# Small tiles of an attention and feed-forward kernel declared in another order, so that the transposed activations lie 64 bytes past the weight slots modulo 256

## Chip, cores and metric

One core of a Trainium2 chip runs the whole program. The metric is the device time of one execution in microseconds (us). Engines are named as in the profile: PE is the matmul engine and PEld its loading of stationary operands, DVE the vector engine, ACT the scalar engine, POOL the GpSimd engine, SP the engine that issues most DMAs. The on-chip memory (SBUF) has 128 partitions; a tile takes the same byte range in each of them, and "address" below is the byte within a partition.

## What is computed

The input x has 2048 rows of 640. It is layer-normed, goes through a local attention and a feed-forward network side by side, and the two are multiplied and added to x:

```python
x = A_x
xn = _layernorm(x, axis=-1)
s = _A_ref(xn, A_wqkv, A_wo)         # 32 heads of 20; each row looks at itself and 7 rows back, step 2
g = _silu(_B_ref(xn, B_w1, B_w2))    # silu(silu(xn @ w1) @ w2), w1 640x1536, w2 1536x640
return x + s * g
```

Attention is `softmax(q . k * 20**-0.5) . v` over 8 positions, then a product with `wo` (640x640); `wqkv` is 640x1920. All is float32.

## The kernel before

**Precision by halves.** Every matmul operand is split into a high and a low half of type fp32r, and each product is made as three matmuls: high by high, low by high, high by low. So one 128x128 piece of a stationary operand is loaded, and one row of up to 512 columns is streamed past it (the moving operand), for each of 3357 matmuls. While a matmul streams, the next one's stationary operand is loaded.

**Staging.** The 2048 rows are taken in four groups of 512 (`groups`), each of four tiles of 128 rows. For each group, PE does these phases in turn:

- `qkv_phase`: four quarters of heads. Per quarter 5 chunks `c` x 4 tiles `t` x 3 matmuls (lines 737 to 739): stationary is a 128-column slice of the transposed normed rows (`TH`, high, or `TL`, low), moving is a slot of the weight ring, 512 columns in three quarters and 384 in the last. In the first group the first quarter is done by `first_quarter` (line 676).
- `wo_phase` for the group before (lines 766 and 768, in `tm_mm`): stationary is a slice of `TH`/`TL`, which now hold the transposed attention output; moving is a weight slot, 384 columns and then 256. That is 120 matmuls. For the last group `wo_last` does it at the end, with 120 matmuls again (15 of them on line 864).
- `ffn_phase`: six times two `up` (lines 882 to 884, 15 matmuls each: stationary is a 128-column piece of a weight slot, moving a whole row of `TH`/`TL`, 512 columns) and one `down` (lines 766 and 768 again, 48 matmuls of 384 and 256 columns: stationary is a slice of `SH` or `SL`, the halves of silu's result, moving a weight slot).

So `TH`/`TL` are stationary in the QKV and `wo` phases and moving in `up`; the weight ring is the other operand everywhere.

**Other engines.** ACT copies matmul results out of PSUM (lines 525, 528), makes silu (888, 889) and exp (588), and copies transposed rows into place (487) and into their high half (471). DVE does the attention itself (571, 574, 609, 614), the low halves (472, 890) and layer norm. POOL issues the loads of already split weights into the ring of 7 slots (line 402), SP the other DMAs. The order of work on ACT, DVE, POOL and SP comes from a planner (`Weave`) that gives every operation a cost and writes one fixed order; no tile's address enters into it. PE's order is that of the code.

**Where tiles lie.** All SBUF tiles come from one pool with one buffer, and are laid one behind the other in the order of their declaration, from address 16512 on; each starts at a multiple of 32 bytes. A slice of 128 columns of `TH` or `SH` begins at a multiple of 512 bytes within its tile, a row `c` of `TH` at a multiple of 2048, a weight slot's low half at 2048, 2560 or 1536; the slots lie 5120 bytes apart. Modulo 256 all pieces of a tile thus start where the tile starts.

Of the kernel before, what the change touches and what calls it, by code (L numbers as in the profile page):

```python
# [8 lines left out]
F32 = mybir.dt.float32  # L9
# [5 lines left out]
P = 128  # L15
S, D, F, H, DH = 2048, 640, 1536, 32, 20
W = 8
# [3 lines left out]
HQ = H // NQ  # L21
CQ = HQ * DH
J = 8
T = 4
# [29 lines left out]
def tsl(t):  # L54
    return slice(t * P, (t + 1) * P)
# [157 lines left out]
def local_attention_silu_ffn(ctx: ExitStack, tc: tile.TileContext, x, wqkv, wo, w1, w2, out):  # L213
    nc = tc.nc
    pool = lambda name, bufs, **kw: ctx.enter_context(tc.tile_pool(name=name, bufs=bufs, **kw))
    sb = pool("sb", 1)
# [16 lines left out]
    def tiles(name, n, shape, dtype=F32):  # L233
        return [sb.tile(shape, dtype, name=f"{name}{i}") for i in range(n)]

    ident = sb.tile([P, P], F32, name="ident")
    epst = sb.tile([P, 1], F32, name="epst")
    MV = sb.tile([P, T, 2], F32, name="mv")
    ST = [sb.tile([P, 2, 6], F32, name="st0")]
    TH = tiles("th", 2, [P, DC, TOK], F32R)  # L240
    TL = tiles("tl", 2, [P, DC, TOK], F32R)
    WR = tiles("w", RING, [P, 2 * D], F32R)
    ST.append(sb.tile([P, 2, 6], F32, name="st1"))
    SH = tiles("sh", 2, [P, TOK], F32R)
    SL = tiles("sl", 2, [P, TOK], F32R)
    SD = sb.tile([P, 2, T], F32, name="sd")
    mask = sb.tile([P, T, W], F32, name="mask")
    M = tiles("m", 2, [P, T, HQ])
    Z = tiles("z", 2, [P, 2, T, HQ])
    KV = tiles("kv", NQ, [P, 2, HALO + T, CQ])  # L250
    Q = sb.tile([P, T, D], F32, name="q")
# [36 lines left out]
    def dve(n, fn, reads, writes, prio, lock=False):  # L288
        add("DVE", dv(n), fn, reads, writes, prio, lock)

    def act(n, fn, reads, writes, prio, table=None):
        add("ACT", ac(n), fn, reads, writes, prio, table=table)

    def pe(dur, fn, reads, writes):
        add("PE", dur, fn, reads, writes)
        clock[0] += dur
# [49 lines left out]
    def width(u):  # L346
        return qcols(u[1]) + 2 * CQ if u[0] == "q" else D
# [41 lines left out]
    def w_load():  # L389
# [5 lines left out]
        n = width(u)  # L395
        r = WR[s]
        both = r[:, :2 * n]
# [27 lines left out]
    def w_next(*want):  # L425
# [4 lines left out]
        s, n = i % RING, width(want)  # L430
        return WR[s][:, :n], WR[s][:, n:2 * n], ("wh", s), ("wl", s)

# [10 lines left out]
    def ln_stats(t, after=()):  # L443
        st = ST[t % 2]
        ks = ("st", t % 2)
        for k in range(2):
            dve(320, lambda k=k: nc.vector.bn_stats(out=st[:, k, :], in_=XIN[:, t, k * 320:(k + 1) * 320]),
                [("xin", t), *after], [ks + (k,)], 1)
        dve(60, lambda: nc.vector.bn_aggr(out=MV[:, t, :], in_=st), [ks + (0,), ks + (1,)], [("mv", t)], 1)

    def ln_rstd(a, b, at=1, after=()):
        n = range(a, b)
        act(b - a, lambda: nc.scalar.activation(SD[:, 0, a:b], MV[:, a:b, 1], AF.Sqrt, bias=epst, scale=1.0),
            [("mv", t) for t in n] + list(after), [("sd", t) for t in n], 0, "sqrt")
        dve(10, lambda: nc.vector.reciprocal(out=SD[:, 1, a:b], in_=SD[:, 0, a:b]),
            [("sd", t) for t in n], [("rs", t) for t in n], at)

    def ln_apply(t):
        dve(320, lambda: nc.vector.tensor_scalar(
            out=XIN[:, t, :], in0=XIN[:, t, :], scalar1=MV[:, t, 0:1], scalar2=SD[:, 1, t:t + 1],  # L460
            op0=OP.subtract, op1=OP.mult), [("rs", t), ("mv", t)], [("xin", t)], 1, lock=True)
# [3 lines left out]
    def split_sb(c, keys, i, prio=0.4):  # L465
# [3 lines left out]
        kh, kl = t_keys(i, [c], kinds=["th"]), t_keys(i, [c], kinds=["tl"])  # L469
        hi, lo = (w[i][:, c, :].rearrange("p (t i b) -> p t i b", t=T, i=NB) for w in (TH, TL))  # L470
        act(TOK, lambda: nc.scalar.activation(hi, v, AF.Copy), keys, kh, prio)
# [84 lines left out]
    def halo_keys(q, ws=(0, 1)):  # L556
        return [("halo", q, tag, a, w) for tag in (1, 2) for a in (0, 112) for w in ws] + [
            ("halo", q, 3, 0), ("halo", q, 4, 0)] + [("kv", q, t) for t in range(T)]
# [4 lines left out]
    def scores(g, q):  # L563
        i = q % 2
        l, e, m, kv, qq = L[i], E[i], M[i], KV[q], Q[:, :, q * CQ:(q + 1) * CQ]
        hk = halo_keys(q, (0,))
# [54 lines left out]
    def first_quarter(i):  # L621
# [10 lines left out]
        def begin(t):  # L632
# [3 lines left out]
            for k in range(2):  # L636
                cs = slice(k * 320, (k + 1) * 320)
                kx = ("xin", t) if t or k else ("xin", t, "a")
                dve(320, lambda k=k, cs=cs: nc.vector.bn_stats(out=st[:, k, :], in_=XIN[:, t, cs]), [kx], [ks + (k,)], at)
            dve(60, lambda: nc.vector.bn_aggr(out=MV[:, t, :], in_=st), [ks + (0,), ks + (1,)], [("mv", t)], at)  # L640
            ln_rstd(t, t + 1, at)
            for j, (a, b) in enumerate(PARTS if not t else ((0, DC),)):
                cs = slice(a * P, b * P)
                dve((b - a) * (64 if not t else 85), lambda cs=cs: nc.vector.tensor_scalar(
                    out=XIN[:, t, cs], in0=XIN[:, t, cs], scalar1=MV[:, t, 0:1], scalar2=SD[:, 1, t:t + 1],
                    op0=OP.subtract, op1=OP.mult), [("rs", t), ("mv", t), ("xin", t)], [("xn", t, j)] if not t else [("xn", t, 0), ("xn", t, 1)],
                    at, lock=True)

        def turn(t):
# [10 lines left out]
            for a, b, j, tp, kp in parts:  # L660
                v = tp[:, :(b - a) * P].rearrange("p (c n) -> p c n", n=P)
                dve((b - a) * P, lambda a=a, b=b, v=v: nc.vector.tensor_tensor(
                    out=TL[i][:, a:b, tsl(t)], in0=v, in1=TH[i][:, a:b, tsl(t)].bitcast(F32), op=OP.subtract),
                    [kp] + t_keys(i, range(a, b), [t], ["th"]), t_keys(i, range(a, b), [t], ["tl"]),
                    1.6 if a and not t else 0)

        def products(t, steps):

            o, kp = ps[t]
            for k, c in steps:  # L670
                x, kx = (TL, "tl") if k == 1 else (TH, "th")
                wh, wl, kh, kl = ws[c]
# [45 lines left out]
    def qkv_phase(g, i, io):  # L718
# [4 lines left out]
        for q in range(NQ):  # L723
            if g == 0 and q == 0:
                ps = first_quarter(i)
            else:
                ps = [bank() for t in range(T)]
                for c in range(DC):
                    wh, wl, kh, kl = w_next("q", q, c)
                    n = width(("q", q, c))  # L730
                    for t in range(T):
                        o, kp = ps[t]

                        def unit(c=c, t=t, o=o, wh=wh, wl=wl, n=n):
                            o = o[:, :n]
                            hi, lo = TH[i][:, c, tsl(t)], TL[i][:, c, tsl(t)]
                            nc.tensor.matmul(o, hi, wh, start=c == 0, stop=False)  # L737
# [16 lines left out]
    def t_keys(i, cs, ts=range(T), kinds=("th", "tl")):  # L754
        return [(k, i, c, t) for k in kinds for c in cs for t in ts]
# [6 lines left out]
    def tm_mm(banks, t, st, w, first, last, cols=(0, 1)):  # L762
        a, b = banks
        h = t % 2
        if 0 in cols:
            nc.tensor.matmul(a[t][0][:, :CA], st, w[:, :CA], start=first, stop=last)  # L766
        if 1 in cols:
            nc.tensor.matmul(b[t // 2][0][:, h * CB:(h + 1) * CB], st, w[:, CA:], start=first and h == 0,  # L768
                             stop=last, skip_group_check=True)
# [18 lines left out]
    def wo_phase(g, i):  # L788
        banks = tm_banks(True)
        a, b = banks  # L790
        for c in range(DC):
# [6 lines left out]
            for t in range(T):  # L798
                def small(c=c, t=t, wh=wh):
                    tm_mm(banks, t, TL[i][:, c, tsl(t)], wh, False, c == DC - 1)  # L800
                pe(TM, small, t_keys(i, [c], [t], ["tl"]) + [kh], [a[t][1], b[t // 2][1]])
# [13 lines left out]
    def wo_last(g, i):  # L815
# [21 lines left out]
        def steps(cs):  # L837
            return [(TH, c, k) for c in cs for k in (0, 1)] + [(TL, c, 0) for c in cs]

# [139 lines left out]
```

## Time and profile before

| | |
|---|---|
| time, median of 3 runs | 621.21 us (621.16 to 621.39) |
| the profiled execution's own time | 621.44 us |
| its span, first to last instruction | 619.7 us |
| PE busy, share of the span | 614.2 us, 99% |
| DVE busy | 561.3 us, 91% |
| ACT busy | 309.5 us, 50% |
| POOL busy | 112.8 us, 18% |
| granted PE clock | 0.999 |

The span is what instructions cover; the 1.7 us between it and the execution's time lie around it. A matmul's busy time in the profile overlaps with that of its neighbours (a 512-column one shows 389 ns, but the next one starts some 227 ns later), so what one matmul costs is read from starts: the start of a phase's first matmul, the start of the next phase's first, and the count of matmuls between.

### The profile page before, as it was taken

Reading aid. Unit: us, or ns where it says so; the run is one execution under the profiler, and the core shown is the slowest. Engines: PE = TensorE matmul, PEld = TensorE weight load, DVE = VectorE, ACT = ScalarE, POOL = GpSimd, SP = SyncE. Lnnn points to the kernel's source line nnn. Section 1 sums busy time; section 2 is a strip of 40 time slices with the busy share of each in tenths; the row PEclk is TensorE's granted clock in tenths of the full one; section 3 lists DMA queues with packets and bytes.
Section 4 is the critical chain, followed back from the end, with each engine's and each line's share of the span. In section 5 each row is a group of like instructions: output and inputs, shape, how many; then the busy total and the mean of one; then the engine's idle time right before and its main releaser. Section 6 shows DMA issues by size and latency. Waiting matters only on the chain.

```text
span 619.7 us, 9092 instructions
## 1 busy us (share of the span) xinstructions
PE 614.2 (99%) x3357; PEld 555.3 (90%) x3357; DVE 561.3 (91%) x581; ACT 309.5 (50%) x651; POOL 112.8 (18%) x168
## 2 busy tenths in 40 slices
PE   8999999999999999999999999999999999999997
PEld 7889999998889999999888999999888999998997
DVE  6558999999989997999998999999979999899974
ACT  5435558937376213951944502583396316152750
POOL 4510000011101133111212233311121213311100
PEclk9999999999999999999999999999999999999999
DMA  8999999866999998764699999855579998956642
GB/s 248 343 287 324 354 345 391 356 236 186 304 322 348 328 356 259 238 195 139 203 242 251 340 333 304 276 176 163 169 202 278 251 334 277 316 179 202 206 124 103
DMA packets 65449, 162.45 MB, mean 262 GB/s; under 512 B 7053, under 2 KB 29165, under 8 KB 65405
## 3 DMA queue, kind: packets, MB, share of 16 engines
q0 software_dynamic: 20016, 82.58, 44.6%
q1 hardware_dynamic: 45389, 79.29, 40.6%
q8 instruction: 26, 0.43, 0.3%
q14 instruction: 18, 0.15, 0.1%
HBM read 109.55 MB, written 34.16 MB: 232 GB/s over the span
## 4 chain that ended last, share of the span: by engine, by line
PE 98%; SPq 1%; DMA 0%; DVE 0%; issue 0%
PE acc L766 22%; PE acc L768 15%; PE acc L737 10%; PE acc L739 10%; PE acc L738 10%; PE rot L883 9%; PE rot L884 9%; PE rot L882 9%; PE acc L676 2%; PE rot L768 1%; DMA pr<-in_A_wqkv_dram 0%; PE rot L766 0%; SPq L376 0%; PE acc L864 0%; SPq L377 0%; PE rot L654 0%
## 5 line engine op out<-in xcount | busy, mean ns | idle before, releaser
L739 PE MATMUL acc<-w,th 128*128 128x512 f32 (+1 forms) x300 | 112.4, 375 | 0.0
L738 PE MATMUL acc<-w,tl 128*128 128x512 f32 (+1 forms) x300 | 112.4, 375 | 0.0
L737 PE MATMUL acc<-w,th 128*128 128x512 f32 (+1 forms) x300 | 112.4, 375 | 0.0
L766 PE MATMUL acc<-w,sh 128*128 128x384 f32 x384 | 111.7, 334 | 0.0
L768 PE MATMUL acc<-w,sh 128*128 128x256 f32 x384 | 107.1, 279 | 0.0
L888 ACT ACTIVATE sh<-rot 128x512 fp32r<-128x512 f32 x48 | 28.6, 597 | 154.2 <-PE rot L884 154.2
L884 PE MATMUL rot<-th,w 128*128 128x512 f32 x240 | 93.8, 391 | 0.0
L883 PE MATMUL rot<-tl,w 128*128 128x512 f32 x240 | 93.8, 391 | 0.0
L882 PE MATMUL rot<-th,w 128*128 128x512 f32 x240 | 93.5, 389 | 0.0
L571 DVE TENSOR_TENSOR pr<-q,kv 128x2560 f32<-128x2560 f32 x32 | 90.2, 2819 | 1.2 <-DMA raw<-in_A_wqkv_dram 1.0
L609 DVE TENSOR_TENSOR pr<-e,kv 128x2560 f32<-128x2560 f32 x32 | 90.3, 2823 | 0.7
L574 DVE TENSOR_REDUCE l<-pr 128x128 f32<-128x2560 f32 x32 | 90.1, 2815 | 0.5
L614 DVE TENSOR_TENSOR pr<-pr 128x1280 f32<-128x1280 f32 x64 | 74.0, 1156 | 1.5
L402 POOL DMA_DIRECT2D w<-half_w x72 | 38.5, 534 | 190.1 <-PE acc L768 94.0
L766 PEld LDWEIGHTS acc<-w,sh 128*128 128x128 f32 x384 | 72.1, 188 | 1.1
L768 PEld LDWEIGHTS acc<-w,sh 128*128 128x128 f32 x384 | 72.2, 188 | 0.9
L402 POOL DMA_DIRECT2D w<-half_q x52 | 27.6, 531 | 238.8 <-PE rot L884 113.5
L737 PEld LDWEIGHTS acc<-w,th 128*128 128x128 f32 x300 | 56.3, 188 | 8.6
L739 PEld LDWEIGHTS acc<-w,th 128*128 128x128 f32 x300 | 56.3, 188 | 8.6
L738 PEld LDWEIGHTS acc<-w,tl 128*128 128x128 f32 x300 | 56.3, 188 | 8.6
L487 ACT ACTIVATE xin<-sf 32x256 f32<-32x256 f32 (+1 forms) x144 | 54.6, 379 | 9.7 <-DVE sf L514 8.0
L766 PE MATMUL acc<-w,sl 128*128 128x384 f32 x192 | 56.1, 332 | 0.0
(104 smaller groups left out, 1059.5 us busy)
## 6 DMA issues: line engine op xcount, KB each, us to landing
w<-half_w POOLq DMA_DIRECT2D x72, 640.0 KB, 6.1
w<-half_q POOLq DMA_DIRECT2D x39, 512.0 KB, 4.3
half_w<-w SPq DMA_DIRECT2D x24, 640.0 KB
w<-half_wo POOLq DMA_DIRECT2D x15, 640.0 KB, 5.6
kv<-kv SPq DMA_DIRECT2D x15, 560.0 KB
half_q<-w SPq DMA_DIRECT2D x15, 512.0 KB
kv<-kv SPq DMA_DIRECT2D x15, 420.0 KB
gate<-in_B_w_dram SPq DMA_DIRECT2D x16, 320.0 KB
```

The lines of the kernel that those rows point to most:

```text
L571: dve(2560, lambda t=t: nc.vector.tensor_tensor(out=PR, in0=win(qq[:, t:t + 2, :], W, 0), in1=win(kv[:, 0, t:t + 2, :], W, CQ), op=OP.mult ...
L574: dve(2560, lambda t=t: nc.vector.tensor_reduce(out=l[:, t:t + 2].rearrange("p t w h -> p (t w h)"), in_=PR.rearrange("p t w (h d) -> p (t ...
L609: dve(2560, lambda t=t, v=v: nc.vector.tensor_tensor(out=PR.rearrange("p t w (h d) -> p t (w h) d", d=DH), in0=e[:, t:t + 2].rearrange("p ...
L614: dve(2 * k * CQ, lambda k=k: nc.vector.tensor_tensor(out=PR[:, :, 0:k, :], in0=PR[:, :, 0:k, :], in1=PR[:, :, k:2 * k, :], op=OP.add), [] ...
L737: nc.tensor.matmul(o, hi, wh, start=c == 0, stop=False)
L738: nc.tensor.matmul(o, lo, wh, start=False, stop=False)
L739: nc.tensor.matmul(o, hi, wl, start=False, stop=c == DC - 1)
L766: nc.tensor.matmul(a[t][0][:, :CA], st, w[:, :CA], start=first, stop=last)
L768: nc.tensor.matmul(b[t // 2][0][:, h * CB:(h + 1) * CB], st, w[:, CA:], start=first and h == 0, stop=last, skip_group_check=True)
L882: nc.tensor.matmul(h, wh[:, cs], TH[i][:, c, :], start=c == 0, stop=False)
L883: nc.tensor.matmul(h, wh[:, cs], TL[i][:, c, :], start=False, stop=False)
L884: nc.tensor.matmul(h, wl[:, cs], TH[i][:, c, :], start=False, stop=c == DC - 1)
```

## The change

Four small tiles are declared at other places: `mask` and the first `m` ahead of, or near, the large tiles, `epst` and `mv` behind `TL`, the second `m` where both were.

```diff
     ident = sb.tile([P, P], F32, name="ident")
-    epst = sb.tile([P, 1], F32, name="epst")
-    MV = sb.tile([P, T, 2], F32, name="mv")
+    mask = sb.tile([P, T, W], F32, name="mask")
     ST = [sb.tile([P, 2, 6], F32, name="st0")]
     TH = tiles("th", 2, [P, DC, TOK], F32R)
     TL = tiles("tl", 2, [P, DC, TOK], F32R)
+    epst = sb.tile([P, 1], F32, name="epst")
+    MV = sb.tile([P, T, 2], F32, name="mv")
+    M = tiles("m", 1, [P, T, HQ])
     WR = tiles("w", RING, [P, 2 * D], F32R)
     ST.append(sb.tile([P, 2, 6], F32, name="st1"))
     SH = tiles("sh", 2, [P, TOK], F32R)
     SL = tiles("sl", 2, [P, TOK], F32R)
     SD = sb.tile([P, 2, T], F32, name="sd")
-    mask = sb.tile([P, T, W], F32, name="mask")
-    M = tiles("m", 2, [P, T, HQ])
+    M.append(sb.tile([P, T, HQ], F32, name="m1"))
     Z = tiles("z", 2, [P, 2, T, HQ])
```

`mask` (128 bytes) in place of `epst` and `mv` (32 each) pushes `st0`, `TH` and `TL` up by 64 bytes; `epst`, `mv` and the first `m` (192 bytes together) then push the weight ring and silu's halves up by 256 in all. From the second `m` on nothing moves. The addresses in the built programs:

| tile | before | modulo 256 | after | modulo 256 |
|---|---|---|---|---|
| `th0`, first of `TH`, `TL` | 17152 | 0 | 17216 | 64 |
| `tl1`, last of them | 47872 | 0 | 47936 | 64 |
| `w0`, first weight slot | 58112 | 0 | 58368 | 0 |
| `w6`, last weight slot | 88832 | 0 | 89088 | 0 |
| `sh0`, first of silu's halves | 94016 | 64 | 94272 | 64 |
| `sl1`, last of them | 100160 | 64 | 100416 | 64 |
| `mask` | 102240 | 96 | 17024 | 128 |
| `epst` / `mv` | 17024 / 17056 | 128 / 160 | 58176 / 58208 | 64 / 96 |
| `m0` | 102368 | 224 | 58240 | 128 |

No instruction is added, taken away or moved: on every engine the built program has the same instructions in the same order with the same waits, and only the addresses of operands differ.

## Prediction

> **What bounds the kernel now.** I read the page first: busy shares, then the chain that ended last.
>
> ```profile
> PE 614.2 (99%) x3357; PEld 555.3 (90%) x3357; DVE 561.3 (91%) x581; ACT 309.5 (50%) x651; POOL 112.8 (18%) x168
> PEclk9999999999999999999999999999999999999999
> PE 98%; SPq 1%; DMA 0%; DVE 0%; issue 0%
> ```
>
> 98% of the chain is PE, at full granted clock, so the time is the sum over 3357 matmuls of the distance from one start to the next. DVE at 91% is the only engine that could take over. Next, the timeline of PE at the phase borders of the last full group:
>
> ```profile
> 446.95 0.40 PE L737 MATMUL acc<-w,th 128*128 128x512 f32 x1
> 487.80 0.33 PE L737 MATMUL acc<-w,th 128*128 128x384 f32 x1
> 498.23 0.33 PE L766 MATMUL acc<-w,th 128*128 128x384 f32 x1
> 515.82 0.40 PE L882 MATMUL rot<-th,w 128*128 128x512 f32 x1
> 522.67 0.34 PE L766 MATMUL acc<-w,sh 128*128 128x384 f32 x1
> 529.56 0.40 PE L882 MATMUL rot<-th,w 128*128 128x512 f32 x1
> ```
>
> The first column is the start, and each row opens a phase. Three QKV quarters (180 matmuls of 512 columns) take 40.85 us, or 226.9 ns each; the fourth (60 of 384) 10.43, or 173.8; `wo` (120, half of 384 and half of 256) 17.59, or 146.6; two `up` (30 of 512) 6.85, or 228.3; `down` (48, half of 384 and half of 256) 6.89, or 143.5. From 512 to 384 columns QKV loses 53.1 ns, that is 0.415 ns a column, so 226.9 holds 212.4 of columns and 14.5 on top: each matmul pays a surcharge with its weight load.
>
> The surcharge is not the same everywhere. `wo` and `down` run the same two lines (766, 768), the same widths, the same moving operand (a weight slot at 0 modulo 256). They differ in where the next stationary piece lies: `TH`/`TL` at 0, `SH`/`SL` at 64. `down` is cheaper by 146.6 - 143.5 = 3.0 ns (unrounded 146.58 - 143.54) a matmul, or by 0.4 us over 120. Higher address bits don't explain it: phases in other slots and in the other `TH` buffer take the same, for instance `up` in the second group,
>
> ```profile
> 213.06 0.40 PE L882 MATMUL rot<-th,w 128*128 128x512 f32 x1
> 219.91 0.34 PE L766 MATMUL acc<-w,sh 128*128 128x384 f32 x1
> ```
>
> 6.85 us again, though slots lie 5120 bytes apart and pieces 512 or 2048.
>
> **The change part by part.** No instruction comes, goes or moves; only addresses change. I price the distance "next stationary minus current moving operand, modulo 256". Today it is 0 in QKV, `wo` and `up`, and 64 in `down`.
>
> *`wo`, 480 matmuls (three phases and `wo_last`).* The distance becomes 64, with the moving operand still at 0: the constellation of `down`, same lines and widths. Price 3.0 ns by the rows above: 480 x 3.0 = 1.44 us. Ends: 0, if silu's halves are cheaper for a reason other than address, and 1.44.
>
> *QKV, 900 matmuls.* Stationary `TH`/`TL` go to 64, the moving slot stays at 0, so the roles are as in `wo`. The surcharge comes once per weight load and is about the same at all widths, so I take 3.0 ns for 512 columns too: 2.70 us. Ends: 0 and 2.70. One doubt goes into the chances: modulo 512 the distance is 320 here and in `wo`, in `down` 64, and today's other phases show only 0 modulo 512.
>
> *`up`, 720 matmuls.* Here the roles are swapped: the moving `TH`/`TL` go to 64, the next stationary slot stays at 0, so the distance is minus 64, or 192. No row shows that constellation. If what counts is that the two streams lie in different 64-byte quarters of 256, it gains 3.0 ns as well, 2.16 us; if the order counts, it may cost as much. Ends +2.16 and -2.16; I take the gain, since `down` is the only row with unequal places, and the nearest.
>
> *`first_quarter`, 60 matmuls:* its starts wait for the first weights, so nothing is counted, at most 60 x 3.0 = 0.2 us.
>
> *`down`, 1152 matmuls:* slots and halves move by 256 together: 0.
>
> *Small tiles.* `mask`, `m0`, `epst` and `mv` are read by short DVE and ACT operations, such as
>
> ```profile
> 254.96 0.42 DVE L581 TENSOR_TENSOR l<-l,mask 128x256 f32<-128x256 f32 x1
> ```
>
> Even a tenth more or less on the eight of these is 0.3 us of DVE, off the chain: 0.
>
> *Weight loads.* They land in slots that stay multiples of 256.
>
> ```profile
> w<-half_w POOLq DMA_DIRECT2D x72, 640.0 KB, 6.1
> ```
>
> A load may take until its slot's next use, six units later; the shortest unit is 12 matmuls of the last quarter, 12 x 173.8 ns = 2.1 us, so 12.5 us against 6.1. A percent faster PE leaves that cover: 0.
>
> A rule stands against all of this. The Trainium skill ("TensorE: Matmul & The Clock Gate", section "Step-by-step: what each phase is for") says that PE has two independent read ports into SBUF, one for the streaming operand and one for the weights. Taken at its word, no distance between the two could matter, and the sum would be 0 and the time 621.2. The trace disagrees by the 3.0 ns between `wo` and `down`, unless something other than address makes that difference.
>
> *What PE runs into when it is earlier.* The sum is 1.44 + 2.70 + 2.16 = 6.3 us. It counts only if what PE waits for comes earlier too. The waits say that ACT follows PE; the long idle times before its work are
>
> ```profile
> ACT sh L888 <- PE rot L884: 154.2, 39, 18.5
> ACT kv L525 <- PE acc L739: 39.5, 12, 8.0
> ```
>
> so silu and the evacuations move with PE. DVE runs one fixed order in which a low half of silu (890) stands every few operations, and that waits for ACT, hence for PE:
>
> ```profile
> 60.00:595.00 535.00, 535.00 (x2942) 484.56 (x2941) 510.33 (x482) 274.37 (x573) 95.41 (x151) 1.00 0.87 266
> 534.33 0.69 DVE L890 TENSOR_TENSOR sl<-sf,sh 128x512 fp32r<-128x512 f32 x1 [2.53 <-ACT sf L889]
> ```
>
> (columns of the first: stretch, its length, busy time of PE, PEld, DVE, ACT, POOL). DVE idles 535.00 - 510.33 = 24.7 us there, four times what it has to give up. There is one place after the start where PE waits already:
>
> ```profile
> 262.82 0.60 ACT L888 ACTIVATE sh<-rot 128x512 fp32r<-128x512 f32 x1
> 263.32 0.28 PE L768 MATMUL acc<-w,sh 128*128 128x256 f32 x1
> 263.47 0.44 PE L766 MATMUL acc<-w,sh 128*128 128x384 f32 x1
> ```
>
> PE's matmul at 263.47 starts just after ACT ends at 263.42; that silu stands behind a run of copies, an exp and two table loads on ACT, which began behind an earlier silu and so come forward nearly as PE does. For this and for places like it I take off 0.3 us (estimate: twice the 0.15 us that PE loses there today).
>
> Sum: 6.3 - 0.3 = 6.0 us. The profiled execution took 621.44 us (span 619.7), so 615.4; the median of the runs is 0.2 lower, 621.21, and 6.0 off that is **615.2 us**.
>
> **The rivals.** A change within 0.2%, 1.24 us, can't be told from none.
>
> 1. *`up` neither gains nor loses:* 6.3 - 2.16 = 4.1 off, 617.1 us. For it: no row with the roles swapped. Against it: if an equal place is what costs, `up` has it today.
> 2. *`up` pays for the minus sign what the others gain:* 4.14 - 2.16 = 2.0 off, 619.2 us.
> 3. *DVE holds PE back.* Its last free run starts at 534.33 after 2.53 us idle, and the chain from it ends in the high halves that `wo_last` needs:
>
> ```profile
> 599.16 1.15 ACT L471 ACTIVATE th<-xin 128x512 fp32r<-128x512 f32 x2
> 600.90 0.34 PE L766 MATMUL rot<-w,th 128*128 128x384 f32 x1
> ```
>
> The first of the two copies ends about 599.8, 1.1 us before its use. If nothing before 531.8 on DVE came forward, PE could be earlier by 2.53 + 1.1 = 3.6 there, plus 0.3 from the some 100 matmuls left: 3.9 off, 617.3 us. Against it: DVE's earlier idle time is spread over the whole run.
> 4. *No effect:* silu's halves are cheaper for another reason, or the ports' rule holds: 621.2 us. Against it: equal code and widths.
> 5. *Slower:* `up`'s swapped roles cost more than all else gains. It decides for slower from (4.14 + 1.24) / 720 = 7.5 ns a matmul on; with 10 ns, 7.2 - 4.1 = 3.1 more, 624.3 us. For it: at 15.9 ns (228.3 - 512 x 0.415) `up` has the highest surcharge already. Against it: that is more than twice the only difference any row shows.
> 6. *`up` gains twice the price:* 2.16 more, 613.0 us.
>
> **How the numbers follow.** Forecast 0.40 (its own range 614.2 to 616.2), `up` neutral 0.20, `up` losing 0.12, DVE holding back 0.09, no effect 0.09, slower 0.06, `up` twice 0.04. The range 613.4 to 619.9 leaves out the last three, 0.19. Faster by over 0.2% (below 619.97): 0.40 + 0.20 + 0.09 + 0.04 and two thirds of 0.12, 0.81; the same: 0.09 and the rest of 0.12, 0.13; slower 0.06.
>
> **What would show it.** In the profile after: `wo` shrinks from 17.59 to about 17.2 us, three QKV quarters from 40.85 to 40.3, the fourth from 10.43 to 10.25, two `up` from 6.85 to 6.76, and `down` stays at 6.89; PE stays above 98% of the chain. `up` at 6.85 or above would show rivals 1 or 2; phases shortened while PE waits for ACT L471 or DVE L890 would show rival 3; `wo` at 17.59 would show that address was not what made `down` cheaper, and with that the whole sum falls.

## The result and the profile after

The changed kernel is slower: 630.14 us (629.81 to 632.17), against 621.30 (621.16 to 621.71) for the kernel before, a ratio of 1.014 [1.0123, 1.0158]. The forecast was 615.2 us with a range to 619.9; the sign is wrong. The profiled execution took 629.82 us, 8.4 more than the 621.44 before, and its span 628.1, 8.4 more than 619.7.

Busy shares, granted clock and the chain of the page after:

```profile
PE 622.6 (99%) x3357; PEld 558.1 (89%) x3357; DVE 562.4 (90%) x581; ACT 309.4 (49%) x651; POOL 112.1 (18%) x168
PEclk9999999999999999999999999999999999999999
PE 99%; DVE 0%; ACT 0%; issue 0%; POOL 0%; POOLq 0%
```

PE is still the whole chain, at full clock. PE's waits after (who waits for whom: us in total, times, longest):

```profile
PE rot L628 <- POOL ident masks.py:199: 1.4, 1, 1.4
PE acc L677 <- ACT w L411: 0.3, 1, 0.3
```

Nothing else is listed for PE, and both stand at the start. (The wait of 0.15 us that the prediction showed at 263.47 is too short for this list; the `down` that holds it takes 0.05 us more than its like now.) So the 8.4 us lie between starts of matmuls that hardly wait. The timeline of PE at the borders of the last full group (first column the start; line numbers are one higher than before: 738 is the first QKV matmul, 767 the first of `wo` and `down`, 883 the first of `up`):

```profile
453.56 0.39 PE L738 MATMUL acc<-w,th 128*128 128x512 f32 x1
495.56 0.34 PE L738 MATMUL acc<-w,th 128*128 128x384 f32 x1
505.96 0.33 PE L767 MATMUL acc<-w,th 128*128 128x384 f32 x1
523.16 0.39 PE L883 MATMUL rot<-th,w 128*128 128x512 f32 x1
530.05 0.34 PE L767 MATMUL acc<-w,sh 128*128 128x384 f32 x1
537.23 0.40 PE L883 MATMUL rot<-th,w 128*128 128x512 f32 x1
544.23 0.34 PE L767 MATMUL acc<-w,sh 128*128 128x384 f32 x1
551.12 0.39 PE L883 MATMUL rot<-th,w 128*128 128x512 f32 x1
```

Three QKV quarters take 42.00 us (40.85 before), the fourth 10.40 (10.43), `wo` 17.20 (17.59). Two `up` take 6.89, then 7.00; `down` 7.18, then 6.89: phases with the same code and the same widths alternate between two times. The sums of all starts by phase, before and after, over the whole trace:

| phase (matmuls) | before, us | after, us | difference |
|---|---|---|---|
| QKV, 512 columns (660) | 149.74 | 153.99 | +4.25 |
| QKV, 384 columns (240) | 41.70 | 41.69 | 0 |
| `up`, 512 (720) | 164.29 | 166.55 | +2.26 |
| `down`, 384 and 256 (1152) | 165.61 | 168.94 | +3.33 |
| `wo` and `wo_last`, 384 and 256 (465) | 68.59 | 67.11 | -1.48 |
| the start, and the last 15 of `wo_last` | 24.42 | 24.47 | +0.05 |

The column adds up to 8.4 us, the difference of the spans. One term of the prediction came true almost to the digit (`wo`), one has the wrong sign (QKV at 512 columns), and the largest surprise is `down`, whose two operands moved together.

Two theories stood at first. Theory A: what counts is the distance between stationary and moving operand modulo 256, with a price that differs by width. Theory B: the place of the weight ring itself (moved by 256, from 256 to 0 modulo 512) costs. `down` speaks against a plain A, since its distance didn't change.

### The profile page after: what moved, and what is told of

Its sections match the earlier page's. It is cut to its first block, busy times and chain, and to the rows that moved or that the text cites. A ratio compares the mean times of both kernels' runs of the same rounds, so it can differ in the third digit from the quotient of the medians.

```text
span 628.1 us, 9092 instructions
## 1 busy us (share of the span) xinstructions
PE 622.6 (99%) x3357; PEld 558.1 (89%) x3357; DVE 562.4 (90%) x581; ACT 309.4 (49%) x651; POOL 112.1 (18%) x168
## 4 chain that ended last, share of the span: by engine, by line
PE 99%; DVE 0%; ACT 0%; issue 0%; POOL 0%; POOLq 0%
PE acc L767 22%; PE acc L769 15%; PE acc L740 10%; PE acc L739 10%; PE acc L738 10%; PE rot L883 9%; PE rot L885 9%; PE rot L884 9%; PE acc L677 2%; PE rot L628 1%; PE rot L769 1%; PE rot L767 0%; PE rot L655 0%; PE acc L865 0%; ACT w L411 0%
## 5 line engine op out<-in xcount | busy, mean ns | idle before, releaser
L739 PE MATMUL acc<-w,tl 128*128 128x512 f32 (+1 forms) x300 | 114.0, 380 | 0.0
L738 PE MATMUL acc<-w,th 128*128 128x512 f32 (+1 forms) x300 | 114.0, 380 | 0.0
L740 PE MATMUL acc<-w,th 128*128 128x512 f32 (+1 forms) x300 | 113.9, 380 | 0.0
L767 PE MATMUL acc<-w,sh 128*128 128x384 f32 x384 | 113.7, 338 | 0.0
L883 PE MATMUL rot<-th,w 128*128 128x512 f32 x240 | 95.0, 396 | 0.0
L885 PE MATMUL rot<-th,w 128*128 128x512 f32 x240 | 94.8, 395 | 0.0
L767 PE MATMUL acc<-w,sl 128*128 128x384 f32 x192 | 57.4, 338 | 0.0
```

Of the source, the lines that this page charges most:

```text
L739: nc.tensor.matmul(o, lo, wh, start=False, stop=False)
L740: nc.tensor.matmul(o, hi, wl, start=False, stop=c == DC - 1)
L883: nc.tensor.matmul(h, wh[:, cs], TH[i][:, c, :], start=c == 0, stop=False)
L885: nc.tensor.matmul(h, wl[:, cs], TH[i][:, c, :], start=False, stop=c == DC - 1)
```

## The experiments

Distances below are "start of the stationary piece minus start of the moving one, modulo 256". All pieces of a tile are alike there, so the runs can't tell the next stationary piece from the current one.

### The ring's place alone: e1_ring256

`TH`/`TL` stay where they were; ring and halves move by 256, as in the change.

```diff
     TL = tiles("tl", 2, [P, DC, TOK], F32R)
+    mask = sb.tile([P, T, W], F32, name="mask")
+    M = tiles("m", 1, [P, T, HQ])
     WR = tiles("w", RING, [P, 2 * D], F32R)
```

(`epst` and `mv` stay ahead of `TH`.)

> TH and TL stay where they were (0 modulo 256); only the weight ring and silu's halves go up by 256, as in the changed kernel. Theory A (what costs is the distance between the next stationary piece and the current moving operand, which is unchanged here): 621.2 us within 0.6, QKV 226.9 ns a matmul of 512 columns, wo 146.6, down 143.5 in every phase. Theory B (the ring's new place, 0 instead of 256 modulo 512, is what costs): slower than before by 4 us or more, with the phases of down alternating between 143.5 and 149.7 ns as in the changed kernel.

Measured: 621.40 us (10 runs), ratio 0.9994 [0.9977, 1.0011]; the kernel before had a median of 622.05 on this chip. The timeline (lines two higher than before) is from a run of 623.20 us, in which PE waits 1.3 us for DVE in the first `down`:

```profile
448.69 0.40 PE L739 MATMUL acc<-w,th 128*128 128x512 f32 x1
489.53 0.33 PE L739 MATMUL acc<-w,th 128*128 128x384 f32 x1
499.96 0.33 PE L768 MATMUL acc<-w,th 128*128 128x384 f32 x1
517.55 0.40 PE L884 MATMUL rot<-th,w 128*128 128x512 f32 x1
524.40 0.34 PE L768 MATMUL acc<-w,sh 128*128 128x384 f32 x1
```

40.84, 10.43, 17.59 and 6.85 us, as before. Theory B falls.

### The rows' place alone: e2_th64_only

`TH`/`TL` go to 64; ring and halves move by 512, so that they stand at the same bytes modulo 512 as before.

```diff
-    epst = sb.tile([P, 1], F32, name="epst")
-    MV = sb.tile([P, T, 2], F32, name="mv")
+    mask = sb.tile([P, T, W], F32, name="mask")
 ...
+    epst = sb.tile([P, 1], F32, name="epst")
+    MV = sb.tile([P, T, 2], F32, name="mv")
+    M = tiles("m", 1, [P, T, HQ])
+    Z = tiles("z", 1, [P, 2, T, HQ])
     WR = tiles("w", RING, [P, 2 * D], F32R)
```

> TH and TL go up by 64; the weight ring and silu's halves go up by 512, so that they lie modulo 512 as in the kernel before. The distance of stationary to moving is 64 modulo 512 here, not 320 as in the changed kernel. Theory A (distance modulo 256 decides): 630 us within 1, QKV 233.3 ns a matmul of 512 columns, wo 143.4, down alternating. Theory B (the ring's place, or the distance modulo 512, decides): 615 us within 1.5, the time that was predicted for the change, with QKV near 224 ns and down at 143.5 throughout.

Measured: 629.71 us (629.67 to 629.84), ratio 1.0116 [1.009, 1.0143].

```profile
523.02 0.39 PE L884 MATMUL rot<-th,w 128*128 128x512 f32 x1
529.90 0.34 PE L768 MATMUL acc<-w,sh 128*128 128x384 f32 x1
537.09 0.40 PE L884 MATMUL rot<-th,w 128*128 128x512 f32 x1
544.08 0.34 PE L768 MATMUL acc<-w,sh 128*128 128x384 f32 x1
550.97 0.39 PE L884 MATMUL rot<-th,w 128*128 128x512 f32 x1
```

6.88, 7.19, 6.99, 6.89: the pattern of the changed kernel, with the distance 64 modulo 512 where the change has 320. So the 64 bytes of `TH`/`TL` are the cause and the ring's own place is not, and the doubt about modulo 512 is settled: it makes no difference.

### Other distances: e3_th192 and e4_th128

The same with `TH`/`TL` at 192 (`mask` and `m0` ahead of them, shown below) and at 128 (`mask` ahead, `epst` and `mv` kept there).

```diff
-    epst = sb.tile([P, 1], F32, name="epst")
-    MV = sb.tile([P, T, 2], F32, name="mv")
+    mask = sb.tile([P, T, W], F32, name="mask")
+    M = tiles("m", 1, [P, T, HQ])
     ST = [sb.tile([P, 2, 6], F32, name="st0")]
```

> As the changed kernel, but TH and TL at 192 modulo 256, so that the signs swap: the next stationary piece lies 64 before the moving operand in QKV and wo, 64 behind it in up. Theory A1 (the order counts, whatever the width): QKV and wo now pay what up paid in the changed kernel (231.3 ns on average for 512 columns) and up what QKV paid (233.3): 630 us within 2. Theory A2 (it is 512 columns that pay when the places differ, in either order): QKV and up both near 231 to 233, wo at 143.4: 630 to 632 us. Theory B (ring): also above 626.

> As the changed kernel, but TH and TL at 128 modulo 256, where both orders have the same distance. Theory A1 and A2 (unequal places cost at 512 columns): slower than before, 626 to 634 us; if cost grows with the distance, above the 630 of the changed kernel. Theory of the prediction (streams in different quarters don't collide): 615 us within 1.5. Theory B (ring): above 626.

Measured: 633.66 us, ratio 1.0186 [1.0151, 1.0221], at 192; 632.45 us, 1.016 [1.0115, 1.0205], at 128. Timeline of the kernel at 192:

```profile
455.88 0.40 PE L739 MATMUL acc<-w,th 128*128 128x512 f32 x1
497.10 0.34 PE L739 MATMUL acc<-w,th 128*128 128x384 f32 x1
507.49 0.34 PE L768 MATMUL acc<-w,th 128*128 128x384 f32 x1
525.09 0.40 PE L884 MATMUL rot<-th,w 128*128 128x512 f32 x1
532.09 0.34 PE L768 MATMUL acc<-w,sh 128*128 128x384 f32 x1
539.28 0.40 PE L884 MATMUL rot<-th,w 128*128 128x512 f32 x1
```

QKV 41.22, `wo` 17.60, `up` 7.00 in every phase and `down` 7.19 in every phase. Here `up` has distance 64 and QKV 192, the reverse of the change, and the prices are swapped: 512 columns at 64 cost 233 ns in whichever phase stands there. It isn't the roles of the tiles. A1 and A2 both set the time too low: neither had `wo` without a gain and `down` at 7.19 throughout. Timeline at 128:

```profile
506.20 0.34 PE L768 MATMUL acc<-w,th 128*128 128x384 f32 x1
524.20 0.39 PE L884 MATMUL rot<-th,w 128*128 128x512 f32 x1
531.17 0.33 PE L768 MATMUL acc<-w,sh 128*128 128x384 f32 x1
538.05 0.39 PE L884 MATMUL rot<-th,w 128*128 128x512 f32 x1
```

`wo` 18.00, `up` 6.97, `down` 6.88. Three kernels with the same `down` (same code, same distance 64) show it at 6.88 throughout, at 7.19 throughout, or in turn. So distance alone doesn't set the price; what runs ahead has a part. That became theory S (a state is handed on) against theory W (distance and width alone).

### Single matmuls: m1_scan

A program of matmuls alone, in series: widths in turn, start `m` of the moving operand, start `s` of the stationary one (in the program both are byte offsets turned into columns of one tile), with 12 matmuls of 512 columns at distance 0 ahead of nearly every series.

```python
for k in range(count):
    w = widths[k % len(widths)]
    nc.tensor.matmul(a[:, :w], X[:, s:s + 128], X[:, m:m + w], start=k == 0, stop=k == count - 1, skip_group_check=True)
```

> Not the reference's computation: x is copied to the output, and beside it PE runs 1986 matmuls without any wait on one SBUF tile, in cases of 24 with a set width (512; 384; 384 and 256 in turn) and a set distance of the stationary piece to the moving operand (0 to 240 bytes in steps of 16), each case after 12 matmuls of 512 columns at distance 0. Only the starts in the trace count. Theory A1 (distance modulo 256 and width decide): 512 columns at 0, 64, 128, 192 cost about 226.7, 233.3, 233.3 and 229 ns as in the QKV phases of the kernels so far, 384 and 256 in turn 146.7, 143.4, 149.9 and 146.7 a matmul; the same distance with both operands moved by 64, or with 256 more, costs the same. Theory S (what ran just before also decides): 384 and 256 in turn at distance 64 cost 143.4 after some cases and 149.8 after others, with the same addresses. The prediction's theory (any unequal place is 3 ns cheaper than 0): every distance of 64 and more near 223.5 ns at 512 columns.

Measured, ns from start to start over the second half of each series:

| distance | 512 columns | 384 and 256 in turn ("the pair") | 384 |
|---|---|---|---|
| 0 | 226.67 | 146.83 | 173.33 |
| 16 | 226.67 | 146.67 | |
| 32 | 233.42 | 146.58 | 173.67 |
| 48 | 232.83 | 143.33 | |
| 64 | 233.17 | 143.42 | 174.58 |
| 96 | 233.75 | 146.75 | 173.67 |
| 128 | 233.17 | 143.25 | 175.92 |
| 144 | 226.67 | 150.00 | |
| 192 | 228.92 | 146.67 | 173.67 |
| 240 | 226.67 | 145.83 | |

The distances left out lie between 229 and 234 ns, between 144 and 151, and at 177. 64 bytes make the 384/256 pair 3.4 ns cheaper and 512 columns 6.5 ns dearer. Only the difference counts, in the few cases tried: `m` = 64 with `s` = 128 takes 233.42 ns as 0 with 64 does. No distance is below 226.67 at 512 columns: the kernel before already stood at the best place for them. The Trainium skill ("TensorE: Matmul & The Clock Gate", section "Step-by-step: what each phase is for") gives the streaming operand and the weights independent read ports; taken at its word, each column of this table would hold one value, and 226.67 against 233.75 disagrees. Two results speak against theory W. The pair at 128 takes 143.25 here, where 149.9 was expected from e4's `wo` at the same distance (150.0). And one series broke it within this program: the pair at 64 takes 143.42 ns after 512 columns, but 150.00 after a pair at distance 0.

### What is handed on: m2_history

> Not the reference's computation: x is copied to the output, and PE runs 2246 matmuls without waits, in series that differ in widths and in the start of the moving operand (m) and of the stationary one (s) modulo 256; 12 matmuls of 512 columns at distance 0 stand between series where a fresh start is wanted. Question: does the step from start to start depend on distance and widths alone (theory W), or also on what ran before (theory S)? S: widths of 384 and 256 in turn at distance 64 take 143.4 ns a matmul after 512 or 384 columns and 150.0 after such a pair at distance 0, and the changed kernel's cycle (384 columns at 64, then four times 30 of 512 columns with m = 64, s = 0 and 48 of 384/256 at distance 64) shows its two kinds of phase again: 512 columns at about 229.5 and 233.3 ns in turn, 384/256 at 149.7 and 143.5. With the 512 columns at distance 0 instead: 226.7 and 143.4 each time. W: one value per series wherever it stands: the same for all four of the cycle, 143.4 for every 384/256 at 64. Series of a kernel with distance 64 in the output projection alone (36 of 512 and 60 of 384 columns at 0, 120 of 384/256 at 64, 30 of 512 at 0, 48 of 384/256 at 64): by S and W 226.7, 173.3, 143.4, 226.7, 143.4, unless 384 columns at 0 hand on the costly state, then 150. Last, 512 columns at 4 to 28, 136 to 152, 236 to 252 bytes: 226.7 up to some byte between 16 and 32, and near 144 and 240; else 233.

The stretches below are the eight phases of the changed kernel's cycle, each from its first start to the next one's (length, then PE's busy time with the matmuls that touch the stretch, neighbours included: 30 and 48 start in it; then the granted clock, the DMA's share and GB/s):

```profile
149.76:156.64 6.88, 6.88 (x32) 1.00 0.00 0
156.64:163.83 7.19, 7.19 (x50) 1.00 0.00 0
163.83:170.82 6.99, 6.99 (x33) 1.00 0.01 2
170.82:177.71 6.89, 6.89 (x50) 1.00 0.00 0
177.71:184.59 6.88, 6.88 (x32) 1.00 0.00 0
184.59:191.78 7.19, 7.19 (x50) 1.00 0.01 2
191.78:198.78 7.00, 7.00 (x33) 1.00 0.00 0
198.78:205.66 6.88, 6.88 (x50) 1.00 0.00 0
```

6.88, 7.19, 7.00, 6.89 and again: the changed kernel's `up` and `down` to the hundredth, from a program of matmuls alone, with no other engine, no wait and no weight arriving. Theory S holds. `down` has two steady patterns, 143.4 and 150.0 ns a matmul. In the cheap one the steps are about 171 and 116 ns in turn, in the dear one 182 and 118. `up` at 192 (64 before the moving operand) leads from one to the other: behind 384 columns at 64 or the cheap pattern it takes 229.4 and the `down` after it is dear, behind the dear pattern it takes 233.2 and the `down` after it is cheap. With 512 columns at 0 between, `down` is at 143.4 each time. The way in is delicate: the pair at 64 takes 150.0 after 2 members of a pair at 0, 143.3 after 4, 150.0 after 8. Two forecasts missed. The pair at 64 takes 150.0, not 143.4, behind 24 of 384 columns, be these at 0 or at 64. And 512 columns don't keep 226.7 from 0 to 16 bytes or around 144 and 240: 4 bytes take 231.92, 8 take 230.83, 12 take 226.67, 20 take 233.25, 28 take 226.67, and 136 and 148 take 233.

The last part was a forecast for a better kernel, and an unwelcome one: after 60 matmuls of 384 columns at 0, the pair at 64 ran its 120 matmuls at 149.96.

The trace before already held a sign of this. Within one `up` there (the first and the last row also stand in the prediction),

```profile
515.82 0.40 PE L882 MATMUL rot<-th,w 128*128 128x512 f32 x1
517.91 0.39 PE L882 MATMUL rot<-th,w 128*128 128x512 f32 x1
522.67 0.34 PE L766 MATMUL acc<-w,sh 128*128 128x384 f32 x1
```

the first 9 matmuls take 2.09 us, 232 ns each, and the other 21 take 4.76, 226.7 each, all at distance 0. So the 228.3 ns that the prediction read as the highest surcharge of all phases is 226.7, as in QKV, and a slow beginning that comes from the phase ahead: behind other 512 columns at 0, m1_scan has 226.67 from the first matmul on.

### The output projection alone at 64: e5_wo64

Each `TH`/`TL` buffer gets 64 bytes more and two views; the normed rows use the first, the attention output the second. Small tiles and padding between the buffers let each start at 0 modulo 256, and the identity matrix lies in `o`; neither is shown in the diff.

```diff
+    def views(t):
+        return [t[:, o:o + ROW].rearrange("p (c n) -> p c n", c=DC) for o in (0, 16)]
 ...
-                    tm_mm(banks, t, TH[i][:, c, tsl(t)], wh, c == 0, False)
+                    tm_mm(banks, t, THO[i][:, c, tsl(t)], wh, c == 0, False)
```

> The transposed rows get buffers 64 bytes longer, with two views: the normed rows stay at 0 modulo 256 (QKV and up at distance 0, as before the change), the transposed attention output is written to and read from 64 bytes further (wo and wo_last at distance 64). Ring at 0 and halves at 64 modulo 256, as before. Theory S with wo entering the cheap state: QKV 40.85 us for three quarters, wo 17.59 to 17.20, up 6.85, down 6.89; 480 matmuls x 3.1 ns = 1.5 us less than before, 619.8 us, ratio 0.9976. If 384 columns at distance 0 ahead of it hand on the costly state: wo about 18.0, three times 0.4 us and wo_last as much, 622.8 us, ratio 1.0025. If any part of the normed rows' loss comes with buffers 64 bytes longer (not with the address of what is read): up at 6.9 or more, QKV at 41 or more, and 624 us or above.

Measured: 622.36 us, ratio 1.0003 [0.9988, 1.0018].

```profile
447.58 0.40 PE L753 MATMUL acc<-w,th 128*128 128x512 f32 x1
488.43 0.33 PE L753 MATMUL acc<-w,th 128*128 128x384 f32 x1
498.86 0.34 PE L782 MATMUL acc<-w,th 128*128 128x384 f32 x1
516.86 0.40 PE L898 MATMUL rot<-th,w 128*128 128x512 f32 x1
```

QKV is back at 40.85, and `wo` takes 18.00: 150.0 ns a matmul, as in the series. `wo_last`, which follows a cheap `down`, went down to 143.4 in the 90 matmuls where its widths alternate. Three times +0.4 and once -0.3 is +0.9 us; the interval doesn't tell that from nothing. The changed kernel's `wo` phases, at 17.20, owed that to what ran ahead as well.

### Other ways in: m3_entry

60 matmuls of 384 columns at 0, a few others, then 48 of the pair at 64:

> Not the reference's computation: x is copied to the output, and PE runs 4103 matmuls without waits. Each series starts with 12 of 512 columns and 60 of 384 at distance 0 (the end of the QKV phase as it was before the change) and ends with 48 of 384 and 256 columns in turn at distance 64 (the output projection at 64); between them stand a few others: 1 to 3 of 256 at 64 or 0, 1 to 3 of 384 at 64, 2 to 24 pairs' members at distance 0 or 128, 1 to 4 of 512 at 0 or 64; or the pair is run narrow first. Theory S (two patterns, and which one holds is set by the way in): the plain series takes 150.0 ns, and some of the ways in lead to 143.4 for all 48, with nothing between the two that lasts. If the 384-column series itself forces the costly pattern whatever follows: 150.0 for all of them. Also 48 members at 16, 32, 48, 128, 176 and 208 straight after 384 at 0: by S 143.4, 146.7 or 150, by distance alone what they took after 512 columns (146.7, 146.6, 143.3, 143.3, 146.5, 144.8); and 640 columns as two times 320 at 0 and 64, priced by nothing yet.

| between the two | the pair, ns a matmul |
|---|---|
| nothing | 149.96 |
| 1 / 2 / 3 of 256 columns at 64 | 143.38 / 149.96 / 150.00 |
| 1 / 2 of 256 at 0 | 149.96 / 143.38 |
| 1 / 2 / 3 of 384 at 64 | 143.38 / 149.96 / 143.38 |
| 2, 4, 6, 12, 18 / 24 of the pair at 0 | 150.0 each / 143.38 |
| 1 / 2 / 4 of 512 at 0 | 150.00 / 149.96 / 143.38 |
| 1, 2 of 512 at 64 | 149.96 each |
| 2 / 12 of the pair at 128 | 143.33 / 149.96 |
| 2 / 6 of the pair at 64, narrow first | 143.38 / 143.38 |
| nothing, but narrow first in all 48 | 143.38 |

Every row settles at one of the two values and stays there. Running the 256 columns ahead of the 384 enters the cheap pattern. At other distances, straight after 384 columns at 0, the pair takes what it took in m1_scan within 0.1 ns at 16, 32, 48, 128 and 208 bytes, and 147.71 against 146.50 at 176. So e4's 150.0 at 128 is a second value at that distance, as at 64; which sequence leads to it was not tried. (Two halves of 320 columns take 146.67 at 0 and 146.54 at 64, no gain.)

### Narrow first in the kernel: e6_wo64_narrow, and alone: e7_narrow_only

In `wo_phase` alone the 256 columns go first, with the projection at 64 (e6) and with everything at 0 as before (e7).

```diff
-        if 0 in cols:
+        if 0 in cols and not narrow:
             nc.tensor.matmul(a[t][0][:, :CA], st, w[:, :CA], start=first, stop=last)
 ...
+        if narrow:
+            nc.tensor.matmul(a[t][0][:, :CA], st, w[:, :CA], start=first, stop=last)
```

> The kernel with the output projection alone at distance 64, and in wo_phase each pair now runs its 256 columns ahead of its 384 (wo_last, down, QKV and up keep their order). Theory S: narrow first enters the cheap pattern, as in the series of single matmuls (143.4 ns against 150.0): wo 18.00 to 17.20 us in each of three phases, 2.4 us less than the same kernel with the wide one first; wo_last stays at 143.4 ns, up after wo at 6.81, the rest as before. Against the kernel before: 480 x 3.1 ns = 1.5 us less, 619.8 us, ratio 0.9976. If the way in means nothing between real waits, wo stays at 18.0 and the ratio at 1.000 to 1.002. If the 1.5 us come off the matmul engine but something else holds it, the phases are short and the ratio is still 1.

> The kernel before (all at distance 0), with the 256 columns ahead of the 384 in wo_phase and nothing else changed. It tells whether the order of the two widths is worth something by itself. Theory S: at distance 0 there is one pattern, 146.6 ns, so wo stays at 17.59 us and the ratio at 1.000; if narrow first is cheaper at any distance, wo 17.2, 1.2 us less, ratio 0.998; if dearer, wo 18.0 and 1.002.

Measured, on one chip with one set of runs of the kernel before (621.45 us): e6 619.82 us (12 runs), ratio 0.9972 [0.9959, 0.9985]; e7 621.79, ratio 1.0006 [0.9991, 1.002]. `wo` in e6, then in e7 (start of `wo`, start of `up`):

```profile
497.03 0.28 PE L784 MATMUL acc<-w,th 128*128 128x256 f32 x1
514.23 0.39 PE L900 MATMUL rot<-th,w 128*128 128x512 f32 x1
```

```profile
499.74 0.28 PE L768 MATMUL acc<-w,th 128*128 128x256 f32 x1
517.34 0.39 PE L884 MATMUL rot<-th,w 128*128 128x512 f32 x1
```

17.20 against 17.60 us. Narrow first is worth nothing at distance 0 and 0.8 us a phase at 64 (18.00 in e5). Together they bring the 465 matmuls to 67.10 us against 68.59 (450 at 143.4 ns, and 15 of `wo_last` that run 384 columns alone), 1.5 us, and no other phase moves by more than 0.11 us; the start, where PE waits for its first operands, took 0.45 us less in this execution of e6. This version beats both kernels.

## Why the prediction was wrong

*What bounds the kernel.* Right: PE alone, at full clock, and all 8.4 us lie in steps from start to start. From the forecast, 6.0 us less, to the trace, 8.4 more, it is 14.4 us: 4.25 + 2.70 = 6.95 in QKV, 2.26 + 2.16 = 4.42 in `up`, 3.33 in `down`, less the 0.3 taken off for waits.

*That the distance of the operands sets part of a matmul's cost.* Right; "no effect" (rival 4) falls with e2 and m1_scan. That any unequal place is cheaper than 0 was wrong.

*`wo`, 1.44 us gained.* Right in size, 1.48, but partly by luck: e5 has the same distance, widths and code, and pays 18.00 where the changed kernel pays 17.20.

*QKV, 2.70 us gained.* This is the step of the prediction that failed first, and the largest: "the surcharge comes once per weight load and is about the same at all widths, so I take 3.0 ns for 512 columns too". The price of a distance differs by width, in sign too: at 64, 512 columns lose 6.5 ns, the 384/256 pair gains 3.4 and 384 columns lose 1.3 or, in the kernel, nothing. 660 x 6.5 = 4.3 us, measured +4.25. The two ends given for this term, 0 and 2.70, had left out a loss, though no row excluded one.

*`up`, 2.16 us gained, ends +2.16 and -2.16.* Measured +2.26 us, a loss just past the lower end. "The nearest row" was `down`, of another width. Rival 5 put a slower kernel down to `up`'s swapped roles; e3_th192 shows that roles have no part, and 2.26 us lost there against 4.14 gained elsewhere would still have been a gain.

*`down`, 0: "slots and halves move by 256 together".* Failed: +3.33 us with its own distance untouched. 12 of 24 phases run at 149.7 ns since the `up` ahead of them leaves PE in the other pattern: 576 x 6.1 = 3.5 us. The prediction took a matmul's price as a property of the matmul. Its own evidence, phases that repeat to the hundredth, fits a steady state as well as a fixed price.

*Small tiles, weight loads, waits, DVE.* Costing them at nothing was right: e1 moves the ring, `mask` and `m0` and takes 621.40; e4 leaves `epst` and `mv` in place and is slow all the same. Rival 3 (DVE holds PE) can't be judged here, since PE came later. In e6, 1.5 us earlier at the end, the gain of the matmuls arrived. The 0.3 us taken off for waits was not seen: the `down` with the prediction's wait takes 7.03 us in e6, where PE is 0.8 us ahead at that place, and 7.04 before. What did come in some runs is a wait that the prediction didn't have: in the traces of e1 and e7, PE waits 1.3 and 1.1 us in the first `down` for DVE's low half of silu.

Rebuilt from m1 and m2 alone, QKV at 512 columns, `up` and `down` lose 660 x 6.5 + 360 x 1.3 + 360 x 5.0 + 576 x 6.1 = 4.29 + 0.47 + 1.80 + 3.51 = 10.1 us (`up` against its 228.2 in the same program at 0), where the trace has 4.25 + 2.26 + 3.33 = 9.8. `wo` can't be rebuilt that way: behind 24 of 384 columns at 64, m2_history has the dear pattern, where the kernel, behind 60 of them, has the cheap one.

What stays open is the mechanism: the runs show when two steady patterns exist and which is entered, not what in the memory or in PE makes them. Nor do they give a rule for the way in beyond the cases tried; why the changed kernel's `wo` is cheap stays open too.

## What to carry to other kernels

Where matmuls follow each other without waits, each with its own weight load, the place of the stationary operand against the moving one modulo 256 bytes is worth up to 7 ns a matmul here, and the price has to be measured for each width: a gain at one width says nothing of another. A phase can also change its speed without being touched, by what runs ahead of it, so a repeated price in a trace is evidence for that sequence alone; small programs with the sequence of widths and distances gave `up` and `down` of the changed kernel and `wo` of e5 and e6, while a series with 24 matmuls ahead in place of 60 missed the changed kernel's `wo`. Place tiles by use (here, two views of one buffer), and try the order of widths within a pair, which cost nothing in e7.

## What the runs showed that was not expected

- 512 columns take 226.67 ns from start to start at distances 0, 12, 16, 28, 144, 240, 244 and 252, and 228.9 to 233.75 at the other distances tried; 4 bytes off 0 already cost 5 ns.
- 384 and 256 columns in turn at distance 64 have two steady patterns, 143.4 and 150.0 ns. Each lasted to the end of its series (120 matmuls in e5's `wo`), and one matmul more or less ahead switches between them.
- The kernel before took 621.14 to 624.65 us over 23 runs on one chip, a spread larger than the gain of e6. None of its long runs was traced; in the traces of e1 (623.20 us) and e7 (622.95) one wait of PE for DVE near the start makes up 1.3 and 1.1 us.
